# Routing in groups of 8, 8, 10 and 10 tiles, with earlier row writes and a reordered tail, in an attention and mixture-of-experts kernel

## The chip, the cores and the metric

One core of one Trainium2 chip. The metric is the device time of one execution in microseconds (us), given as the median of a few runs.

## The reference

Linear attention without a softmax, a norm per head, and then a mixture of eight experts that sends each token to one expert:

```python
kv = einsum('bhsd,bhse->bhde', k, v)             # batch 8, heads 8, seq 576, head_dim 64
out = einsum('bhsd,bhde->bhse', q, kv)
rms = sqrt(mean(out * out, axis=-1) + 1e-06)
x = (out / rms * g_norm)                          # reshaped to 4608 tokens x 512
logits = x @ w_gate                               # 8 experts
e_idx = argmax(logits, axis=1)
gate_w = softmax(logits)[e_idx]
eom = sigmoid(x @ w_output_gate)
for e in range(8):                                # w1: 512 x 1024, w2: 1024 x 512
    h = maximum(x[mask_e] @ w1[e], 0)
    out[mask_e] = gate_w * eom[:, e] * (h @ w2[e])
```

## The kernel before

The work has two phases. **Phase 1** is attention, gating and routing; **phase 2** is the experts. On TensorE, ScalarE, VectorE and GpSimd the order of phase 1 is the order of the program text (GpSimd's order is free in phase 2). SyncE issues the loads and the row writes, one behind the other, in program order too.

*Attention.* The 36 token tiles (128 tokens each) come out of eight batches. For a batch, five `kv_step`s (L486) sum k times v in PSUM; `kvT_part` (L510) and `m_part` (L522) fold the gate weights into it, so that one product gives a tile's attention output and its gate products together. `m_part` is the gate product; it writes the PSUM tile `mrp`. `run_out` (L785) makes one token tile: `out_tile` (TensorE, L576), for the tile before it `out_rows` (ScalarE: the row, its squares, the gate products), and for the one before that `sums` (VectorE, L602). Between these it issues loads (`load`, L468) as slots of a pool of 20 come free. Some `constant` matmuls (L484) on ones compute nothing that is used; their numbers stand in `COLD`.

*Routing.* The tiles are taken in groups, `GR`: 16, 10 and 10. When a group's last sum is there, the generator `route` (L614) begins. It has eight steps, each ended by a `yield`: (1) the inverse root of the sums, and on GpSimd its copy into the rows (L639); (2) gate products times it (L647); (3) logits, maximum, one-hot; (4) counts, and matmuls into `mrp` that number the tokens (L683 to L690); (5) two exponentials on ScalarE; (6) each token's slot, its output factor (the reciprocals, L723), and the writing of its rows to the HBM tensor `xs` (`xwrite`, L757 and L762); (7) the operands `la` and `rrc` of the tables (L733 to L739); (8) the table matmuls (L742), whose sum VectorE keeps in `tsum` (L744, L746). `STEPS` says after which token tile a group takes how many steps. Rows are written in chunks: tiles 0 to 7 in one, then two tiles each up to 25, then five and five. `xwrite` holds them back until all loads have been issued.

*The lead.* After 16 tiles the expert with most tokens so far is known. Its first 256 tokens are the lead, run 0: `gather(0)` (L243) reads its rows back from `xs` on GpSimd's queue, `scale_heads` (L259) multiplies in the norms on VectorE, `stage` (L267) transposes them (L283), `lead1` (L300, products at L308) is the first product in eight blocks, and the second is the part of `mm2` at L364. `HOOKS` puts the gather at tile 35. `TAIL` is the order by hand behind the 36 tiles: a digit is one step of that group, L one step of the lead (two tiles staged, then eight blocks), Q the last rows and sums, W the loads of the lead's second weights, C 8 `constant` matmuls, K the order of the other experts. So the last group's routing is interleaved with the lead's first product. Then come `index` (rows of run 1), `split` of the four chunks of the first expert's w1, and `others` (the other experts' rows).

*Experts.* Run 1 is the rest of the first expert, then come the other seven. Weights and tokens are each split into a rounded part and a remainder (`split`: rounded part on ScalarE at L218 or L225, remainder on VectorE at L221 or L228), and three products are summed. `mm1` (L313, matmuls at L329) is the first product in eight hidden blocks f, each emptied by ScalarE (L344) and VectorE (L345); the w2 chunks are split between these blocks. `mm2` (L352, L377 and L383) is the second product, with the next run's row tiles staged in it. Rows of a run are gathered on GpSimd's queue and scaled on GpSimd (L259), and outputs are scattered there (L394). An expert's loop for overflowing tokens at the end finds nothing to do here.

Of the kernel before, what the change touches and what calls it, by code (L numbers as in the profile page):

```python
# [25 lines left out]
E = 8  # L26
# [17 lines left out]

NOVER = NT + E

GR = (16, 10, 10)
GROUPS = [list(range(sum(GR[:i]), sum(GR[:i+1]))) for i in range(len(GR))]
GMAX = max(GR)

# [15 lines left out]

STEPS = [{18: 1, 19: 1, 20: 1, 24: 1, 25: 1, 26: 1, 27: 1, 31: 1},
         {29: 1, 30: 1, 31: 1, 36: 1}, {}]  # L70

PLACES = ['VP', 'VP', 'V']

HOOKS = {35: "G"}
TAIL = "Q11WCCCCLL2L2L2L221L2L1L2KLL2"

COLD = (24, (8, 8, 10, 5), 5, 4, 12, 8)

GPSIMD_GROUPS = 0
APART = (2,)  # L80


NORMS = "VV"

ROUND = 1.5 * 2.0 ** 30

# [39 lines left out]
def tiles_of(i):  # L126

    _, t0, n = RUNS[i]
    return [(t0 + k, k * P, min(P, n - k * P)) for k in range(-(-n // P))]
# [6 lines left out]
def body(ctx: ExitStack, tc: tile.TileContext, kvm, rem, qT, wg, gn, w1, w2, kc, xs, tab, out):  # L136
    nc = tc.nc
# [56 lines left out]
    def wload(p, which, c, eng=None):  # L194
        r = take([P, 1024], F32, "wraw")
        eng = eng or nc.sync
        src = (w1 if which == 1 else w2)[ds(expert(p, eng), 1), c]
        d = eng.dma_start(out=r, in_=src.rearrange("o p x -> p (o x)"))
        raw[(p, which, c)] = r
        return d  # L200
# [35 lines left out]
    xg, tails, xT, hT = {}, {}, {}, {}  # L236
# [19 lines left out]
    def scale_heads(x, eng):  # L256
        v = x[:, 0:DM].rearrange("p (h d) -> p h d", d=D)
        f = x[:, C_RMS:C_RMS + H].unsqueeze(2).to_broadcast([x.shape[0], H, D])
        eng.tensor_tensor(out=v, in0=v, in1=f, op=ALU.mult)  # L259

    def scale_rows(i):
        for k, (t, c0, M) in enumerate(tiles_of(i)):
            if i == 0 and NORMS[k] == "V":
                continue
            scale_heads(xg[(RUNS[i][0], t)][:M], nc.gpsimd)

    def stage(i, k):  # L267
        p = RUNS[i][0]
        t, c0, M = tiles_of(i)[k]
        x = xg.pop((p, t))  # L270
        if i == 0 and NORMS[k] == "V":
            scale_heads(x[:M], nc.vector)
        if k == 0:
            if i == 0:
                xT[i] = take([P, 4, LEAD], F32, "xT")
            else:
                xT[i] = [[mem.tile([P, 4, CMAX], F32R, name="xT", tag=f"xT{j}")] for j in range(2)]
        tl = cst.tile([P, 1], F32, name="tl", bufs=14)
        nc.vector.tensor_copy(tl[:M], x[:M, C_SCALE:C_SCALE + 1])
        tails[(p, t)] = tl  # L280
        ps = ps_b.tile([P, 2, 512], F32, name="tps", tag="big")[:, 0].rearrange("p (c m) -> p c m", c=4)
        for c in range(4):
            nc.tensor.transpose(ps[:, c, :M], x[:M, c * P:(c + 1) * P], ident[:M, :M])  # L283
        give(x)
        if i == 0:
            nc.scalar.activation(xT[0][:, :, c0:c0 + M], ps[:, :, :M], AF.Copy, scale=gcol[:, 0:1])
            return
        for j, (hi, lo) in enumerate(zip(*xT[i])):
            n = hi.shape[1]
            v = ps[:, j * n:(j + 1) * n, :M]  # L290
            nc.scalar.copy(hi[:, :, c0:c0 + M], v)  # L291
            nc.vector.tensor_tensor(out=lo[:, :, c0:c0 + M], in0=v,  # L292
                                    in1=hi.bitcast(F32)[:, :, c0:c0 + M], op=ALU.subtract)
# [107 lines left out]

    def lead_run():

        for k in range(len(tiles_of(0))):
            stage(0, k)
            yield
        for f in range(8):
            lead1(f)
            yield
# [70 lines left out]
    def constant(ps, n, start=True):  # L480

        for _ in range(n):
            k = ps.shape[1] // P
            nc.tensor.matmul(ps, ones, ones.unsqueeze(1).to_broadcast([P, k, P]), start=start, stop=start)  # L484

    def kv_step(b, s):  # L486

        r = rt[b // 2]
        q0 = (b % 2) * 64
        ps = kvp  # L490
        if s < 4 and b == 0:
            constant(ps[:, 256:512], COLD[1][s] + (COLD[0] if s == 0 else 0), s == 0)
        for p in range(NP):
            for u in range(2):
                c = slice(p * P + u * D, p * P + (u + 1) * D)
                if s < 4:
                    k, v = kvt[(b, s)][:, 0, c], kvt[(b, s)][:, 1, c]
                else:
                    k, v = r[q0:q0 + 64, 0, c], r[q0:q0 + 64, 1, c]

                nc.tensor.matmul(ps[u * D:(u + 1) * D, p * D:(p + 1) * D], k, v, start=(s == 0 and p == 0),
                                 stop=(s == 4 and p == NP - 1))
        if s < 4:
            give(kvt.pop((b, s)))
        elif b % 2:
            give(rt.pop(b // 2))
        if s == 4:
            nc.scalar.copy(augs[b % 3][:, :, 0:D], ps[:, 0:NP * D].rearrange("q (p d) -> q p d", p=NP))
# [30 lines left out]
    g = 0  # L539
# [214 lines left out]

    opened = [False, False]

    def xwrite(g, o, i):  # L757
        late = g >= LEAD_TILES
        if not opened[late]:
            xwrites.append((g, o, i))  # L760
            return
        nc.sync.dma_start(out=o, in_=i)  # L762
        if id(i) in held:
            give(i)
# [40 lines left out]
    def act(step):  # L805
        if step.isdigit():
            advance(int(step))
        elif step == "W":
            for c in range(4):
                wload(0, 2, c)  # L810
        elif step == "K":
            ranks()
        elif step == "Q":
            while outs:
                out_rows()
            while squares:
                sums()
        elif step == "G":
            free.extend(rfree)
            rfree.clear()  # L820
            gather(0)
        elif step == "C":
            constant(ps_b.tile([P, 2, 512], F32, name="cps", tag="big")[:, 0, 0:256], COLD[5])
        else:
            next(lead, None)
# [93 lines left out]
    with tc.manual_schedule(engines=MAN):  # L919
        p1_main()  # L920
        index()
        for c in range(4):
            split(0, 1, c)
        others()
    p1.close()

    def overflow_list():
# [67 lines left out]
    with tc.manual_schedule(engines={ET.PE, ET.Activation, ET.DVE}):  # L995
        for i in range(len(RUNS)):
            p = RUNS[i][0]
            T = len(tiles_of(i))
            last_run = i + 1 == len(RUNS)
            change = not last_run and RUNS[i + 1][0] != p  # L1000
            if i == 0:
                gather(1)
                scale_rows(1)
            else:
                for f in range(8):
                    mm1(i, f)
                    if f % 2:
                        split(p, 2, f // 2)
                        drop(1, f // 2)
                        if change:  # L1010
                            wload(p + 1, 1, f // 2)
                    if f == 2 and not last_run:
                        g_ = gather(i + 1)
                        if i + 2 == len(RUNS):
                            settle(g_)
                    if f == 3 and not last_run:
                        scale_rows(i + 1)
                    if i > 1:
                        next(listing, None)
            Tn = 0 if last_run else len(tiles_of(i + 1))  # L1020

            at = {}

            def put(k, f, e, *a):
                at.setdefault(k, {}).setdefault(f, []).append(lambda: e(*a))

            if change:
                for c in range(4):
                    at_ = (c, 0) if T >= 4 else divmod(c * T * 2, 8)
                    put(*at_, split, p + 1, 1, c)  # L1030
                    put(*at_, wload, p + 1, 2, c)
            places = [(k, f) for k in range(T) for f in (2, 5)]
            places = places[-Tn:] if Tn > len(places) - 2 else places[:-1]
            for x in range(Tn if i else 0):
                put(*places[x * len(places) // Tn], stage, i + 1, x)
            order = list(range(T))
            if last_run and half(i):
                order.insert(1, order.pop())
            for k in order:
                g_ = mm2(i, k, at.get(k, {}))  # L1040
                if last_run and k == order[-3]:
                    settle(g_)
            if i == 0:
                for h in hT.pop(0):
                    give(h)
                for k in range(Tn):
                    stage(1, k)
            if i > 0:
                for c in range(4):
                    drop(2, c)  # L1050
# [105 lines left out]
```

## Time and profile before

| | |
|---|---|
| median of 3 runs | 575.64 us (572.77 to 577.5) |
| the profiled execution | 577.09 us |
| its span, first to last instruction | 575.3 us |
| mean granted TensorE clock | 0.975 of full |
| TensorE matmuls busy | 560.7 us, 97% of the span |
| VectorE, ScalarE, GpSimd busy | 251.3, 220.1, 150.0 us |
| moved | 92.25 MB, mean 160 GB/s |
| row writes to `xs` | one of 2112 KB, nine of 528, two of 1320 |

Times are counted from the span's start. "Granted clock" is TensorE's, as a share of its upper level of 2.4 GHz; 0.5 is the lower level, 1.2 GHz. PE is TensorE, DVE VectorE, ACT ScalarE, POOL GpSimd, SPq SyncE's queue. A line such as `L221 DVE ... wlo<-wraw,gcol,whi` names the kernel's line, the engine, and output and inputs by tile names. In a line of the timeline the first two numbers are start and duration in us, `xN` is the number of instructions merged in it, and the bracket is the engine's idle time before it with what seems to have ended it. A busy share of TensorE is not its peak rate, as the ends of matmuls are modelled.

### The profile page before, as it was taken

How to read it: one execution, taken by the hardware profiler on the slowest of the kernel's cores; microseconds unless marked ns; L12 is line 12 of the kernel's file. 1: busy time of each engine (PE TensorE's matmuls, PEld its weight loads, DVE VectorE, ACT ScalarE, POOL GpSimd, SP SyncE). 2: the span in 40 equal slices, each digit the busy share in tenths (PEclk: the TensorE clock that was granted, in tenths of full speed). 3: DMA queues.
4: the chain of work that ended last, by engine and by line, in shares of the span. 5: the costliest groups of instructions: out<-in, count | busy, mean ns of one | idle time of the engine just before them, and what ended most of it. 6: DMA issues, size and time to landing. Idle time of an engine off the chain costs nothing.

```text
span 575.3 us, 10502 instructions
## 1 busy us (share of the span) xinstructions
PE 560.7 (97%) x4220; PEld 489.8 (85%) x4220; DVE 251.3 (44%) x519; ACT 220.1 (38%) x399; POOL 150.0 (26%) x168
## 2 busy tenths in 40 slices
PE   9899989998999999999999999999999999999995
PEld 6798978857988998899889988998799889879974
DVE  2033998872754563154413441353145425424400
ACT  1277765232452344134323432334235324433410
POOL 2000241348327005600450046005500631020011
PEclk9889995998999999999999999999999999999999
DMA  8999997966266223442254234323622443110000
GB/s 278 383 417 417 416 355 254 365 221 210 79 198 202 76 74 119 132 151 76 92 161 142 75 112 160 121 74 111 184 92 83 133 158 114 56 40 18 0 38 29
DMA packets 28739, 92.25 MB, mean 160 GB/s; under 512 B 4081, under 2 KB 4209, under 8 KB 28688
## 3 DMA queue, kind: packets, MB, share of 16 engines
q1 hardware_dynamic: 21952, 71.63, 35.1%
q0 software_dynamic: 6304, 19.70, 10.7%
q8 instruction: 35, 0.57, 0.4%
q10 hardware_dynamic: 432, 0.21, 0.2%
q14 instruction: 16, 0.13, 0.1%
HBM read 72.34 MB, written 19.70 MB: 160 GB/s over the span
## 4 chain that ended last, share of the span: by engine, by line
PE 77%; issue 1%; DVE 1%; ACT 1%; DMA 0%; POOL 0%; POOLq 0%
PE hps L329 34%; PE yps L383 32%; PE yps L377 3%; PE tps L283 3%; PE hps L308 2%; PE yps L364 2%; DVE wlo L228 1%; DMA out<-y,oidx 0%; DVE xT L292 0%; POOL out L394 0%; DVE hT L345 0%; ACT y L393 0%; ACT whi L225 0%; ACT hT L344 0%; POOLq L251 0%
## 5 line engine op out<-in xcount | busy, mean ns | idle before, releaser
L383 PE MATMUL yps<-whi,hT 128*128 128x512 f32 (+3 forms) x560 | 184.9, 398 | 0.0
L329 PE MATMUL hps<-xT,whi 128*128 128x256 f32 (+5 forms) x960 | 178.1, 305 | 0.9 <-ACT xT L291 0.4
L329 PEld LDWEIGHTS hps<-xT,whi 128*128 128x128 f32 x960 | 148.6, 189 | 3.0 <-DVE xT L292 0.6
L383 PEld LDWEIGHTS yps<-whi,hT 128*128 128x128 f32 (+3 forms) x560 | 104.0, 186 | 23.3
L394 POOL DMA_INDIRECT out<-y,oidx x42 | 45.7, 1089 | 258.1 <-ACT y L393 238.6
L383 PE MATMUL yps<-wlo,hT 128*128 128x512 f32 (+3 forms) x280 | 109.9, 393 | 0.0
L329 PE MATMUL hps<-xT,wlo 128*128 128x256 f32 (+5 forms) x480 | 109.7, 304 | 0.0
L345 DVE SCALAR_TENSOR_TENSOR hT<-hps,hT 128x512 fp32r<-128x512 f32 (+5 forms) x104 | 54.7, 526 | 116.8 <-ACT hT L344 116.7
L344 ACT ACTIVATE hT<-hps 128x512 fp32r<-128x512 f32 (+5 forms) x104 | 48.2, 467 | 140.7 <-PE hps L329 105.3
L329 PEld LDWEIGHTS hps<-xT,wlo 128*128 128x128 f32 x480 | 80.2, 189 | 0.4
L383 PEld LDWEIGHTS yps<-wlo,hT 128*128 128x128 f32 (+3 forms) x280 | 52.1, 186 | 10.7
L221 DVE SCALAR_TENSOR_TENSOR wlo<-wraw,gcol,whi 128x1024 fp32r<-128x1024 f32 x32 | 42.3, 1330 | 42.5 <-ACT whi L218 40.6
L259 POOL TENSOR_TENSOR xg<-xg 128x512 f32<-128x512 f32 (+8 forms) x40 | 44.4, 1118 | 38.5 <-DMA xg<-xs,gidx 29.2
L393 ACT ACTIVATE y<-yps,tl 128x512 f32<-128x512 f32 (+3 forms) x37 | 25.5, 689 | 75.5 <-PE yps L383 66.5
L243 POOL DMA_INDIRECT xg<-xs,gidx x42 | 42.1, 1002 | 43.2 <-PE yps L364 15.9
L228 DVE TENSOR_TENSOR wlo<-wraw,whi 128x1024 fp32r<-128x1024 f32 x32 | 41.8, 1307 | 16.9 <-ACT whi L225 14.6
L292 DVE TENSOR_TENSOR xT<-tps,xT 128x512 fp32r<-128x512 f32 (+8 forms) x40 | 25.3, 635 | 45.6 <-ACT xT L291 45.5
L576 PE MATMUL ops<-aug,ld 64*128 64x80 f32 (+1 forms) x640 | 45.2, 305 | 0.0
L291 ACT CAST xT<-tps 128x512 fp32r<-128x512 f32 (+8 forms) x40 | 21.5, 542 | 60.5 <-PE tps L283 60.5
L576 PEld LDWEIGHTS ops<-aug,ld 64*128 64x128 f32 (+1 forms) x640 | 39.8, 207 | 3.4 <-issue 1.5
L602 DVE TENSOR_REDUCE ss<-sq 128x8 f32<-128x512 f32 x36 | 23.9, 681 | 37.7 <-ACT sq L592 37.7
L218 ACT ACTIVATE whi<-wraw,gcol 128x1024 fp32r<-128x1024 f32 x32 | 36.3, 1143 | 0.0
(163 smaller groups left out, 443.2 us busy)
## 6 DMA issues: line engine op xcount, KB each, us to landing
wraw<-w SPq DMA_DIRECT2D x64, 512.0 KB, 3.5
ld<-kvm SPq DMA_DIRECT2D x32, 512.0 KB, 9.9
ld<-qT SPq DMA_DIRECT2D x18, 512.0 KB, 9.9
xs<-xrow SPq DMA_DIRECT2D x9, 528.0 KB, 5.9
xs<-xrow SPq DMA_DIRECT2D x2, 1320.0 KB, 7.8
xs<-xrow SPq DMA_DIRECT2D x1, 2112.0 KB, 9.3
ld<-rem SPq DMA_DIRECT2D x3, 512.0 KB, 9.9
xg<-xs,gidx POOLq DMA_INDIRECT x42, 3.6
```

The lines of the kernel that those rows point to most:

```text
L218: he.activation(hi, r, AF.Copy, scale=gcol[:, 0:1])
L221: eng.scalar_tensor_tensor(out=lo, in0=r, scalar=gcol[:, 0:1], in1=hi.bitcast(F32), op0=ALU.mult, op1=ALU.subtract)
L228: eng.tensor_tensor(out=lo, in0=r, in1=hi.bitcast(F32), op=ALU.subtract)
L243: gathered = nc.gpsimd.indirect_dma_start(out=x[:M, :], out_offset=None, in_=rows, in_offset=bass.IndirectOffsetOnAxis(ap=gidx[:M, p, t:t ...
L259: eng.tensor_tensor(out=v, in0=v, in1=f, op=ALU.mult)
L329: nc.tensor.matmul(ps[:, j, :n], w[:, o:o + P], x[d][:, j * N:j * N + n], start=(d == 0 and k == 0), stop=(d == 3 and k == 2))
L344: nc.scalar.activation(hh, x, AF.Relu)
L345: nc.vector.scalar_tensor_tensor(out=v(h[:, l:l + n]), in0=x, scalar=0.0, in1=hh.bitcast(F32), op0=ALU.max, op1=ALU.subtract)
L383: nc.tensor.matmul(ps[:M], a, b, start=(f == 0 and k == 0), stop=(f == 7 and k == 2))
L393: nc.scalar.activation(y[:M], ps[:M], AF.Copy, scale=tl[:M, 0:1])
L394: i_ = nc.gpsimd.indirect_dma_start(out=out, out_offset=bass.IndirectOffsetOnAxis(ap=oidx[:M, p, t:t + 1], axis=0), in_=y[:M], in_offset=N ...
L576: nc.tensor.matmul(v[r0:r0 + m, u, p, :], qt[g // 2][r, p, q0:q0 + m], augs[b % 3][r, p, :], start=True, stop=True)
```

## The change

The routing groups become 8, 8, 10 and 10. The lead is still made of the first 16 tiles, now the first two groups. The step tables move with that: the third group's first six steps run up to tile 34, before the tail, where the group of the same tiles had four by tile 36; the table matmuls of the first 16 tiles come at tiles 20 and 28 instead of 31. A hook E at tile 19 writes the rows of tiles 0 to 7 without waiting for the loads to be issued, and the lead's gather moves from tile 35 to 34. The last three `kv_step`s of batch 1 get 6, 5 and 3 `constant` matmuls. In the tail the lead's norms stand first, ahead of the last rows and sums, and two C (16 matmuls) replace four (32). `others` comes ahead of `split`, and only two w1 chunks are split there; the other two are split in run 1, behind its hidden blocks 0 and 2.

```diff
-GR = (16, 10, 10)
+GR = (8, 8, 10, 10)
...
-STEPS = [{18: 1, 19: 1, 20: 1, 24: 1, 25: 1, 26: 1, 27: 1, 31: 1},
-         {29: 1, 30: 1, 31: 1, 36: 1}, {}]
-PLACES = ['VP', 'VP', 'V']
-HOOKS = {35: "G"}
-TAIL = "Q11WCCCCLL2L2L2L221L2L1L2KLL2"
-COLD = (24, (8, 8, 10, 5), 5, 4, 12, 8)
+STEPS = [{10: 1, 11: 1, 12: 1, 14: 1, 15: 1, 16: 1, 17: 1, 20: 1},
+         {18: 1, 19: 1, 20: 1, 23: 2, 24: 1, 25: 1, 28: 1},
+         {28: 1, 29: 1, 30: 1, 32: 1, 33: 1, 34: 1}, {}]
+PLACES = ['VP', 'VP', 'V', 'V']
+HOOKS = {19: "E", 34: "G"}
+TAIL = "LCQWLLC3L3L3L332L3L2L3KLL3"
+COLD = (24, (8, 8, 10, 5), 5, 4, 12, 8, (0, 0, 6, 5, 3))
...
-APART = (2,)
-NORMS = "VV"
+APART = (3,)
...
     def lead_run():
+        for t, c0, M in tiles_of(0):
+            scale_heads(xg[(0, t)][:M], nc.vector)
+        yield
         for k in range(len(tiles_of(0))):
             stage(0, k)
             yield
...
     def kv_step(b, s):
+        if b == 1:
+            constant(ps[:, 256:512], COLD[6][s], False)
...
-    def xwrite(g, o, i):
+    def xwrite(g, o, i, wait=True):
         late = g >= LEAD_TILES
-        if not opened[late]:
+        if wait and not opened[late]:
             xwrites.append((g, o, i))
             return
...
+        elif step == "E":
+            for w in [w for w in xwrites if w[0] < 8]:
+                xwrites.remove(w)
+                xwrite(*w, False)
...
         index()
-        for c in range(4):
+        others()
+        for c in range(2):
             split(0, 1, c)
-        others()
...
                 for f in range(8):
                     mm1(i, f)
+                    if i == 1 and f in (0, 2):
+                        split(0, 1, f // 2 + 2)
```

## Rows read from the trace of the kernel before

**Rows 1.** Chain that ended last, in order of time: start, us, what.
```profile
102.96 5.45 PE hps L308 x24
...
118.42 13.82 PE yps L364 x32
...
135.86 6.39 PE hps L329 x23
...
144.58 3.83 DVE wlo L228
...
149.52 7.20 PE hps L329 x36
```
**Rows 2.** Timeline of GpSimd, 80 to 182 us.
```profile
90.83 1.09 POOL L243 DMA_INDIRECT xg<-xs,gidx  x1 [5.88 <-DVE ss L602]
...
92.22 0.95 POOL L243 DMA_INDIRECT xg<-xs,gidx  x1 [0.30 <-issue]
...
122.43 1.04 POOL L243 DMA_INDIRECT xg<-xs,gidx  x1 [15.63 <-PE yps L364]
...
131.52 2.05 POOL L259 TENSOR_TENSOR xg<-xg 128x512 f32<-128x512 f32 x2
...
142.28 7.03 POOL L259 TENSOR_TENSOR xg<-xg 128x512 f32<-128x512 f32 x6
```
**Rows 3.** Timeline of SyncE's queue, the row writes.
```profile
75.08 6.71 SPq L762 DMA_DIRECT2D xs<-xrow  x5
...
111.65 2.63 SPq L762 DMA_DIRECT2D xs<-xrow  x2
```
**Rows 4.** By tile, issue to landing: xs in 70 to 125, xg in 80 to 140.
```profile
DMA to landing us min/median/max: 2.9/5.6/10.1
...
DMA to landing us min/median/max: 3.1/4.4/5.0
```
**Rows 5.** Timeline of VectorE, 85 to 112 us.
```profile
86.54 0.17 DVE L749 CAST gidx<-gif 128x2 int32<-128x2 f32 x1
...
96.28 0.69 DVE L602 TENSOR_REDUCE ss<-sq 128x8 f32<-128x512 f32 x1 [1.02 <-ACT sq L592]
...
98.46 0.67 DVE L259 TENSOR_TENSOR xg<-xg 128x512 f32<-128x512 f32 x1
...
99.77 0.19 DVE L623 TENSOR_SCALAR ra<-ss 128x80 f32<-128x80 f32 x1
...
111.33 0.25 DVE L723 RECIPROCAL xrow<-rdn 128x5 f32<-128x5 f32 x2
```
**Rows 6.** Stretches: length, busy us of engines (instructions), PE clock, DMA share, GB/s.
```profile
74.00:76.00 2.00, 2.00 (x44) 1.85 (x44) 1.90 (x12) 2.00 (x7) 2.00 (x5) 1.00 0.44 175
76.00:92.00 16.00, 14.01 (x230) 12.88 (x230) 15.26 (x42) 10.12 (x25) 4.82 (x9) 0.80 1.03 374
```
**Rows 7.** Groups by line and shape, VectorE, 57 to 104: busy, mean ns | idle.
```profile
L631 DVE SCALAR_TENSOR_TENSOR ru<-ry 128x80 f32<-128x80 f32 x2 | 0.5, 243 | 0.1
...
L631 DVE SCALAR_TENSOR_TENSOR ru<-ry 128x128 f32<-128x128 f32 x1 | 0.3, 294 | 0.0
```
**Rows 8.** Stretches of phase 1 (busy: PE, PEld, DVE, ACT, POOL).
```profile
24.00:34.50 10.50, 10.44 (x136) 9.30 (x136) 2.65 (x4) 6.15 (x15) 0.00 (x0) 0.51 1.02 418
...
40.00:57.00 17.00, 17.00 (x360) 15.30 (x360) 6.38 (x10) 13.33 (x35) 0.00 (x0) 1.00 1.03 416
57.00:80.00 23.00, 23.00 (x495) 20.79 (x495) 22.00 (x63) 17.04 (x45) 7.79 (x13) 1.00 0.97 386
```
**Rows 9.** Waits of TensorE, 0 to 104 us: total, times, longest.
```profile
PE mrp L527 <- DVE tsum L744: 2.0, 1, 2.0
```
**Rows 10.** The stretch behind that wait.
```profile
85.77:95.06 9.29, 9.26 (x104) 8.83 (x105) 8.13 (x24) 6.96 (x16) 2.04 (x2) 0.50 0.99 349
```
**Rows 11.** The two remainder subtractions of weights: duration ns min/median/max, first and last start.
```profile
L228 DVE TENSOR_TENSOR wlo<-wraw,whi x32: 1224/1226/3832, 144.6 to 545.4; 128x1024 fp32r<-128x1024 f32 x32
...
L221 DVE SCALAR_TENSOR_TENSOR wlo<-wraw,gcol,whi x32: 1273/1285/1725, 120.0 to 510.9; 128x1024 fp32r<-128x1024 f32 x32
```

More of the change, by code (lines that the diff above doesn't have):

```diff
@@ L262, in scale_rows @@
         for k, (t, c0, M) in enumerate(tiles_of(i)):
-            if i == 0 and NORMS[k] == "V":
-                continue
             scale_heads(xg[(RUNS[i][0], t)][:M], nc.gpsimd)
@@ L270, in stage @@
         x = xg.pop((p, t))
-        if i == 0 and NORMS[k] == "V":
-            scale_heads(x[:M], nc.vector)
         if k == 0:
```

## The prediction

> **What bounds the kernel now.** I read the granted clock and busy time by stretch first, then the chain that ended last, then the queues of SyncE, GpSimd and VectorE one after the other in time.
>
> From 102.96 us the chain is TensorE with hardly a break: the lead's first product, its second from 118.42 for 13.82, then run 1 from 135.86, and after that the seven other experts [rows 1]. So nearly all of the time lies behind 136 us in matmuls that the change leaves alone. What it can move is the moment at which run 1 starts, and what run 1 then loses. Two breaks show in it: between the lead's end (132.24) and 135.86, and a VectorE subtraction of 3.83 us at 144.58 that the chain passes through [rows 1].
>
> What sets 135.86? Not the lead: GpSimd finishes scaling run 1's last two row tiles at 133.57 (131.52 plus 2.05), after the lead's last matmul [rows 1, 2]. GpSimd began that string (four gathers, four scalings, one output) at 122.43 and never waited in it. The gather at 122.43 needs every token row in HBM. The last two writes leave SyncE at 111.65, right behind the reciprocals that end at 111.58, and row writes land up to 10.1 us after issue [rows 3 to 5]; the second of the two, about a microsecond behind the first, fits that. So run 1 hangs on the last routing group, whose chain on VectorE begins at 99.77 and takes 11.8 us [rows 5]. In front of 99.77 stand the last sum (96.28), the end of the group before, and the lead's norms (98.46) [rows 5].
>
> The lead's own gather leaves at 90.83, though its index is ready at 86.7 [rows 2, 5]. It waits for the first 16 tiles' rows: writes issued from 75.08 for 6.71 us, landing up to 10.1 later [rows 3, 4]. Transfers are the limit there: share 0.44 in 74 to 76, then 1.03 until 92 [rows 6].
>
> **The change part by part.**
>
> *A fourth group.* The 28 or so small operations of a routing chain now run twice for the first 16 tiles. One takes 0.294 us on 128 columns and 0.243 on 80 [rows 7]; on 64 that is about 0.225 by the same slope, so 28 x (0.45 - 0.29) = 4.5 us more on VectorE. They fall at tiles 10 to 20, where VectorE works 6.38 us of 17 [rows 8]: cost 0 on the path, at worst 4.5 if they pile up behind the full stretch from 57 to 80 (22.00 of 23) [rows 8]. That full stretch loses half of the group of 16, by my count of its operations about 5.5 us. VectorE should therefore reach the lead's norms at about 91 to 92 instead of 98.46: 5.5 for this, and 1.3 for two sums that now come later.
>
> *Rows of tiles 0 to 7 at tile 19.* By the slot count only the last two q loads are still behind this write on SyncE; they land 5 to 6 us later, about 80, when tile 32 is due to need them. The bytes only change order, since the queue was full. What is won is the hole at 74 to 76: 2 x (1 - 0.44) = 1.1 us [rows 6]. The lead's gather goes from 90.83 to 89.7. Bounds: 0 (the hole comes back elsewhere) and 5.8, if its 2,112 KB (2.16 MB, at 374 GB/s [rows 6]) found free transfer time.
>
> *Dummy matmuls in batch 1 and the tables moved.* In 24 to 34.5 the clock was 0.51 [rows 8]. If the 14 dummies hold it, TensorE comes 3 to 5 us earlier to the loads, but the loads and the row writes do not end earlier: 0 on the path, bounds -3 and 0. The tables made the gate product wait 2.0 us for a VectorE copy [rows 9], and a stretch at 0.50 followed [rows 10]. Without it the last token tiles come earlier, but the lead's gather still waits for the writes: 0 again. The group before the last is ready by then, so its row writes no longer stand between norms and last group.
>
> *Norms ahead of the last sums, 16 dummies instead of 32.* The second lead gather follows the first by 1.4 [rows 2] and lands a median 4.4 us after issue [rows 4]: 89.7 + 1.4 + 4.4 = 95.5. Behind the waiting norm on VectorE stand the last two sums and the whole last group. Norm 0.67, two sums about 1.3 [rows 5]: the last group begins at 97.5 instead of 99.77, a gain of 2.3. Bounds: 6.0, if data are there and VectorE is the limit (92 + 0.67 x 2 + 1.3, less overlaps, 93.8); -1, if the gather lands at the 5.0 end and VectorE comes late. The lead's products start some 6 us earlier, about 97, which is hidden: run 1 waits for the last group, and TensorE idles before it some 3 us longer.
>
> *Two weight splits moved into run 1.* Before, all four w1 splits ran before run 1 under the lead's second product, and cost nothing. Now chunks 2 and 3 stand between run 1's first hidden blocks, on ScalarE and VectorE, with the product's own evacuations behind them. The subtraction takes 1.285 each [rows 11]. The ScalarE-VectorE chain there was already what TensorE waited for [rows 1], so I take 2 x 1.285 = 2.6 as lost. Bounds: 0 (slack between evacuations takes it) and 7.7 (both stretched as in the row of 3.83). What they free, VectorE and ScalarE time before run 1, only brings the index of run 2 forward, and GpSimd's string never waited for that.
>
> The row of 3.83 stands beside GpSimd's six scalings of 142.28 to 149.31 [rows 2]; the same subtraction's median is 1.226 [rows 11]. The Trainium skill (SBUF — State Buffer, Who interferes with whom) says that a VectorE instruction with two SBUF inputs and a GpSimd one that reads SBUF exclude each other for a whole instruction. By that rule the added subtractions, which also read two tensors, can be held up too, which speaks against the change and is the second rival below.
>
> *Sum.* -2.3 + 2.6 = +0.3. The profiled execution took 577.09 us (span 575.3), 1.45 above the median of the runs, 575.64. It would come to 577.4; by the median, 575.9, rounded 576.
>
> **The rivals.**
>
> A, faster: VectorE, not the gather, sets the last group, because half of the lead's rows were written long before. The last group begins at 93.8, 6.0 earlier, and the gaps between evacuations absorb the two splits: 575.6 - 6.0 = 569.6. For it: 4.3 MB of writes (16 tiles of 264 KB) stood in front of the lead's gather and only half still do. Against: the transfer engines had nothing free before 74, so the other half is not free either.
>
> B, slower: run 1's evacuations fall behind. Each added subtraction meets GpSimd's scaling and takes 3.83 instead of 1.285: 2 x 2.55 = 5.1 on top. TensorE then stands in holes as long as the 2.0 that was followed by 0.50 [rows 9, 10], and at least one hidden block (12 matmuls; 36 take 7.20 [rows 1], so 2.4, with the evacuations' holes left out 2.3) runs at half clock: 575.9 + 5.1 + 2.3 = 583. It decides from the point where two of the three subtractions in that window are held up. For it: one was. Against: GpSimd's string of 7 us is over by the time of the third.
> [...]
>
> C, the change does not do what it says: the norm blocks VectorE until the old landing time, the last group starts at 99.8, and only the splits are felt: 575.6 + 2.6 = 578.2. For it: gather and landing are the least certain times above. Against: the hole in the transfers is really there.
>
> **How the numbers follow.** Forecast 0.43, A 0.26, B 0.16, C 0.15. The forecast's own range is 573 to 579. The whole range takes in A, with a microsecond and a half below it, and most of B: 568 to 582.5. A measurement of this kernel can tell about 1% (5.8 us) from no change. Faster by more than that (under 569.9) is most of A, with a little of the forecast's lower end: 0.27. Slower by more (over 581.4) is B: 0.16. The rest 0.57.
>
> **What would show it.** In the changed kernel the lead's gather should issue near 89.7, its norms start near 94 with VectorE idle in front, the lead's first product near 97, the last group's chain near 97.5, run 1's gather near 120 and its first matmul near 133.5. TensorE should stand for 2 to 3 us in run 1 behind VectorE's evacuations, and batch 1 should show the full clock. I am wrong if run 1 starts before 131 (then A), if run 1's eight blocks take 5 us longer than the 20.9 of now, 135.86 to 156.72 [rows 1] (then B), or if the last group starts at 99 or later (then C).

## The result, and the profile after

| | before | after |
|---|---|---|
| median, same chip, side by side | 573.22 us (20 runs, from 572.71) | 579.01 us (20 runs, from 574.01) |
| profiled execution, its span | 577.09, 575.3 us | 579.98, 578.1 us |
| ratio, 95% interval | | 1.0063 [1.0036, 1.0090] |

The change costs 0.4 to 0.9% by the interval; the forecast was 576.0 (568 to 582.5) and no difference that can be told. The times of after lie at two levels, about 574 to 575 and 578 to 581. One run of the twenty on each side was in a slower state of the chip; medians, here and below, are over all runs, and ratios leave such runs out.

All of the difference lies ahead of run 1's second product: from there to the end of the span it is 418.6 us before (575.3 - 156.72 [rows 1]) and 418.0 after (578.1 - 160.05). The chain of waits of after, start, us, what:

```profile
90.96 7.21 DMA xg<-xs,gidx
98.19 0.69 DVE xg L260
98.88 1.19 DVE ss L604 x2
...
112.52 0.58 PE mrp L744 x10
113.10 5.25 PE hps L305 x24
...
118.78 12.96 PE yps L361 x30
131.76 0.44 ACT y L390
...
135.41 4.01 PE hps L326 x11
...
140.72 1.15 ACT whi L219
141.90 5.54 DVE wlo L222
...
148.54 11.52 PE hps L326 x48
160.05 2.07 PE yps L380 x9
```

Two things are new in it. The lead's gather itself is now on the chain, for 7.21 us, with the norms and the last two sums behind it; and the subtraction of a moved split takes 5.54 us where [rows 11] have 1.285. Run 1's products go on from 135.41 (one matmul at 134.65 stands alone ahead of them, as one at 135.10 did before). Beside [rows 1] (135.86) that is 0.45 earlier, which misleads, as the second experiment shows. The chain comes to run 1 over TensorE: the last group's table matmuls (112.52) stand ahead of the lead's last three blocks and its second product, and run 1 goes on 3.67 us behind the end of that product (131.74); before it was 3.62 (132.24 and 135.86). VectorE's timeline of after, the tail:

```profile
96.45 0.69 DVE L260 TENSOR_TENSOR xg<-xg 128x512 f32<-128x512 f32 x1 [7.25 <-DMA xg<-xs,gidx]
...
98.19 0.69 DVE L260 TENSOR_TENSOR xg<-xg 128x512 f32<-128x512 f32 x1 [1.05 <-DMA xg<-xs,gidx]
...
100.11 0.20 DVE L625 TENSOR_SCALAR ra<-ss 128x80 f32<-128x80 f32 x1
...
107.75 2.04 DVE L735 TENSOR_SCALAR la<-ni,rlon 128x128 bf16<-128x128 f32 x10
...
112.38 0.25 DVE L725 RECIPROCAL xrow<-rdn 128x5 f32<-128x5 f32 x2
```

VectorE reaches the first norm at 89.2 and stands 7.25 us in front of it, then 1.05 more. The last group begins at 100.11, behind the 99.77 of [rows 5]. GpSimd and SyncE's queue in the same time:

```profile
89.57 1.09 POOL L244 DMA_INDIRECT xg<-xs,gidx  x1 [9.87 <-DMA wraw<-w]
...
122.25 0.97 POOL L244 DMA_INDIRECT xg<-xs,gidx  x1 [18.65 <-DVE zf L886]
...
141.30 7.03 POOL L260 TENSOR_TENSOR xg<-xg 128x512 f32<-128x512 f32 x6
```
```profile
79.11 4.42 SPq L199 DMA_DIRECT2D wraw<-w  x4
87.92 4.38 SPq L764 DMA_DIRECT2D xs<-xrow  x5
92.54 4.86 SPq L199 DMA_DIRECT2D wraw<-w  x4
```

The gather leaves at 89.57 (90.83 in [rows 2]), and in front of it and between its two halves SyncE puts the five row writes of the third group, which before came only in the tail. By tile, in 88 to 96, issue to landing of the lead's two gathers of after, beside 4.0 to 4.7 before:

```profile
DMA to landing us min/median/max: 6.9/7.0/7.2
```

Stretches of after (columns as in [rows 6]): there is no hole in the transfers (share 1.04 where it was 0.44), the first stretch of [rows 8] has the full clock, and in the tail the transfers stay full. The first two of these need not be the work of the change: the second experiment shows them without it.

```profile
74.00:76.00 2.00, 2.00 (x51) 1.85 (x48) 1.76 (x10) 0.56 (x2) 0.00 (x0) 1.00 1.04 393
...
85.00:99.80 14.80, 8.36 (x62) 7.19 (x61) 6.37 (x23) 6.10 (x14) 2.04 (x2) 0.62 1.04 400
24.00:34.50 10.50, 9.96 (x210) 8.84 (x210) 3.43 (x5) 8.28 (x21) 0.00 (x0) 1.00 1.03 418
```

### The profile page after: what moved, and what is told of

It is laid out like the page before. It is cut to its first block, busy times and chain, and to the rows that moved or that the text cites. A ratio compares the mean times of both kernels' runs of the same rounds, so it can differ in the third digit from the quotient of the medians.

```text
span 578.1 us, 10543 instructions
## 1 busy us (share of the span) xinstructions
PE 556.8 (96%) x4221; PEld 485.5 (84%) x4221; DVE 259.4 (45%) x557; ACT 219.8 (38%) x401; POOL 142.9 (25%) x163
## 3 DMA queue, kind: packets, MB, share of 16 engines
q1 hardware_dynamic: 21952, 71.63, 34.5%
## 4 chain that ended last, share of the span: by engine, by line
PE 80%; DMA 12%; DVE 4%; issue 1%; ACT 1%; POOL 0%; POOLq 0%; ACTq 0%; DVEq 0%; SPq 0%
PE hps L326 34%; PE yps L380 32%; DMA ld<-kvm 5%; PE yps L374 3%; DMA xs<-xrow 3%; PE tps L280 3%; PE ops L578 3%; PE yps L361 2%; PE kvp L503 2%; DMA wraw<-w 1%; DMA xg<-xs,gidx 1%; DMA gcol<-gn 1%; DVE wlo L222 1%; PE hps L305 1%; DMA out<-y,oidx 0%
## 5 line engine op out<-in xcount | busy, mean ns | idle before, releaser
L222 DVE SCALAR_TENSOR_TENSOR wlo<-wraw,gcol,whi 128x1024 fp32r<-128x1024 f32 x32 | 47.8, 1498 | 43.8 <-ACT whi L219 42.0
L244 POOL DMA_INDIRECT xg<-xs,gidx x42 | 40.8, 971 | 50.1 <-DVE zf L886 18.7
L229 DVE TENSOR_TENSOR wlo<-wraw,whi 128x1024 fp32r<-128x1024 f32 x32 | 39.2, 1225 | 16.9 <-ACT whi L226 13.8
L578 PE MATMUL ops<-aug,ld 64*128 64x80 f32 (+1 forms) x640 | 41.4, 282 | 0.1
L578 PEld LDWEIGHTS ops<-aug,ld 64*128 64x128 f32 (+1 forms) x640 | 36.1, 187 | 3.2 <-issue 1.2
```

The source lines that it names most:

```text
L222: eng.scalar_tensor_tensor(out=lo, in0=r, scalar=gcol[:, 0:1], in1=hi.bitcast(F32), op0=ALU.mult, op1=ALU.subtract)
L229: eng.tensor_tensor(out=lo, in0=r, in1=hi.bitcast(F32), op=ALU.subtract)
L244: gathered = nc.gpsimd.indirect_dma_start(out=x[:M, :], out_offset=None, in_=rows, in_offset=bass.IndirectOffsetOnAxis(ap=gidx[:M, p, t:t ...
L578: nc.tensor.matmul(v[r0:r0 + m, u, p, :], qt[g // 2][r, p, q0:q0 + m], augs[b % 3][r, p, :], start=True, stop=True)
```

## The experiments

Two questions: how much each of the tail's new order and the moved splits costs, and what holds the lead's gather back. Medians below are of runs beside the kernel before on the same chip; the kernel before had 573.3 to 574.5 in them.

**The splits put back (the change's tail alone).** In the changed kernel `range(2)` is `range(4)` again and the two splits in run 1 go.

> The changed kernel with all four w1 splits ahead of run 1 again (after the other experts' rows), nothing else undone. Theory S (the loss is made in run 1, by the two added subtractions, one of which took 5.54 us beside GpSimd's scaling): run 1's first product, from its second matmul to the first of the second product, falls from 24.6 us (135.41 to 160.05) to about 21, and the time by 3 to 4 us, to the level of the kernel before or 0.5 under it, with less scatter. Theory T (the loss is made in the tail of phase 1, where the lead's second gather landed 7.2 us after issue and ten la operations stand on VectorE): run 1 begins where it does now and the time stays within 1 us of the changed kernel.

578.69 us, ratio 1.0088 [1.0063, 1.0114]: nothing is won. Run 1 starts at 136.22, and its chunk of w2 meets the scaling instead, in VectorE's and GpSimd's timelines:

```profile
143.37 6.13 DVE L229 TENSOR_TENSOR wlo<-wraw,whi 128x1024 fp32r<-128x1024 f32 x1 [0.72 <-ACT whi L226]
```
```profile
143.38 7.02 POOL L260 TENSOR_TENSOR xg<-xg 128x512 f32<-128x512 f32 x6
```

So the loss lies in the tail, with or without the moved splits: run 1 starts no earlier, as theory T had it.

**The split moved alone, in the kernel before.**

```diff
-        for c in range(4):
+        for c in range(2):
             split(0, 1, c)
...
+                    if i == 1 and f in (0, 2):
+                        split(0, 1, f // 2 + 2)
```

> The kernel before with the move of two w1 splits into run 1 as its only edit. Theory S: run 1's first product takes 3 to 4 us longer than its 20.9, and the time is 3 to 5 us above the kernel before. Theory T: within 1 us of the kernel before.

576.32 us (575.26 over the nine runs that the ratio counts), ratio 1.0023 [1.0005, 1.0041]: 0.3 to 2.4 us, under theory S's 3 to 5, and not clearly within the 1 of theory T. This kernel has the old tail, untouched, and shows what that does in an execution at the usual clock. Its timelines of VectorE and GpSimd:

```profile
95.50 0.69 DVE L259 TENSOR_TENSOR xg<-xg 128x512 f32<-128x512 f32 x1 [1.64 <-DMA xg<-xs,gidx]
...
96.84 0.19 DVE L623 TENSOR_SCALAR ra<-ss 128x80 f32<-128x80 f32 x1
...
137.12 6.62 DVE L221 SCALAR_TENSOR_TENSOR wlo<-wraw,gcol,whi 128x1024 fp32r<-128x1024 f32 x1 [0.83 <-ACT whi L218]
```
```profile
118.24 1.53 POOL L243 DMA_INDIRECT xg<-xs,gidx  x1 [14.38 <-DMA xs<-xrow]
...
137.60 7.02 POOL L259 TENSOR_TENSOR xg<-xg 128x512 f32<-128x512 f32 x6
```

The last group starts at 96.84 and run 1 at 132.22, not at the 99.77 and 135.86 of the profiled execution of before [rows 1, 5]. That one was some 4 us above its kernel's usual time: its stretch at a clock of 0.50 [rows 10] reads 0.82 here, on the same tail.

```profile
85.77:95.06 9.29, 7.92 (x85) 6.41 (x81) 7.61 (x30) 5.13 (x15) 2.04 (x2) 0.82 0.86 316
```

Beside this, the change starts run 1 3.2 us later (135.41 - 132.22). What remained of the early start here went into run 1's eight blocks, 24.99 us: TensorE waited 3.3 us in them, behind the subtraction of 6.62, and the clock stood at 0.50 from 144 to 150. Two more marks of the profiled execution of before are not found here, without the hook E and without dummies in batch 1:

```profile
24.00:34.50 10.50, 9.47 (x208) 8.43 (x208) 3.43 (x5) 7.32 (x18) 0.00 (x0) 1.00 1.02 415
74.00:76.00 2.00, 2.00 (x41) 1.77 (x39) 1.86 (x5) 1.68 (x5) 0.62 (x1) 1.00 1.04 409
```

So neither the clock of 0.51 in [rows 8] nor the hole at 74 in [rows 6] belongs to every execution of that kernel.

**The norms later.** TAIL "CQW333LLLCLLL332L3L2L3KLL3" puts the last rows, sums and three steps of the last group ahead of the lead's norms.

> The changed kernel with another tail: last rows and sums first, then the first three steps of the last group, and only then the lead's norms, so that VectorE works while it waits for the lead's gather (in the changed kernel it stood 7.25 us and then 1.05 more). Theory N (the norm ahead of the sums holds the last group back): the last group begins near 91 instead of 100.1, its reciprocals end near 106 instead of 112.6, run 1's gather goes near 116 and run 1 is then held by the lead's end, so it begins 1 to 3 us earlier; time 1 to 3 us below the changed kernel. Rival M (transfers hold run 1's gather: row writes land no earlier since the queue is full up to 104): run 1's gather still near 121 or later and the time unchanged.

578.46 us, ratio 1.0069 [1.0048, 1.0090]: no gain. The last group did start at 92.94, but the matmuls that number its tokens stood on TensorE behind the lead's blocks, and its reciprocals came at 111.09 (112.38 in after). Run 1's gather left at 121.69, where the rival had 121 or later, and run 1 started at 136.88, 3.67 us behind the lead's second product again. With the lead's blocks behind the same late gather, the order takes back what it gives.

**No dummies in batch 1.** `COLD[6]` is all zeros.

> The changed kernel without the 14 dummy matmuls of batch 1. The prediction put them at 0 on the path: the clock in 24 to 34.5 falls back to about 0.5, token tiles come up to 3 us later, the lead's gather still issues near 89.6, and the time stays within 1 us of the changed kernel. Rival (the dummies pay): the lead's gather and run 1 begin 2 us or more later and the time rises by that.

579.22 us (575.91 over the nine runs that the ratio counts), ratio 1.0046 [1.0011, 1.0081]. The interval overlaps that of the change: the dummies cost and win nothing that shows in the time. Without them the clock in 24 to 34.5 was 0.51 (before), 1.00 (the split moved alone) and 0.79 (here, in a profiled run of 586.52 us); with them it was 1.00 in all eleven profiles. So the dummies may hold the clock there, which three profiles without them don't settle.

**The third group's rows later.** Its sixth step goes back into the tail, behind the norms.

```diff
-         {28: 1, 29: 1, 30: 1, 32: 1, 33: 1, 34: 1}, {}]
+         {28: 1, 29: 1, 30: 1, 32: 1, 33: 1}, {}]
...
-TAIL = "LCQWLLC3L3L3L332L3L2L3KLL3"
+TAIL = "LCQ2WLLC3L3L3L332L3L2L3KLL3"
```

> The changed kernel, but the third group's sixth step (which issues the row writes of tiles 16 to 25) stands in the tail, behind the lead's norms and the last sums, as the group of the same tiles had it behind the sums. Theory G (these writes and the weight loads behind them share the transfer engines with the lead's gather, which therefore lands 7.2 us after issue instead of 4.4): the gather lands within 5 us, the second norm starts near 96 instead of 98.2, the lead's first product near 99 instead of 101.5, while the last group, which now waits for the sixth step too, begins near 99; run 1 begins no earlier than now, because the later row writes push the last ones back. Time within 2 us of the changed kernel. Rival (the gather is slow for another reason): the second norm still at 98 or later.

577.91 us, ratio 1.0082 [1.0051, 1.0112]; the gathers' landing only falls to 6.0 us, where theory G had 5, the second norm starts at 98.21, as the rival had it, and the last group at 101.76. The row writes leave at 101.63, but two loads of weights slid into their place:

```profile
80.10 7.30 SPq L199 DMA_DIRECT2D wraw<-w  x6
...
101.63 4.40 SPq L764 DMA_DIRECT2D xs<-xrow  x5
```

In this profile run 1's eight blocks took 20.7 us (135.64 to 156.32): no subtraction was stretched, and the first five of GpSimd's scalings took 7.5 us together instead of 5. TensorE had no wait for VectorE in them, so that the forecast's term of 2.6 for the splits is not to be seen there.

**Tables shared with GpSimd.** `PLACES[2]` is 'VP', so that four of the third group's ten `la` go back to GpSimd.

> The changed kernel with the table operands of the third group shared by VectorE and GpSimd, as the group of the same tiles had them; the change put all ten on VectorE. Theory P (the last group's chain on VectorE sets run 1): its reciprocals end 1.0 us earlier after its start (12.5 us now, 11.8 before), and run 1 and the time follow by about 1 us. Rival (the chain's end does not matter): time unchanged within 0.5 us.

579.58 us, ratio 1.0116 [1.0098, 1.0133]. The chain from the group's start to the start of its last reciprocals is 0.87 us shorter (11.40 against 12.27), as theory P had it. But the group began 0.69 us later (100.80), so that run 1's gather left only 0.18 earlier (122.07), and run 1 started at 136.02, 3.61 us behind the lead's second product (132.41). The time is no better; five runs of a kernel with two levels can't tell what the 0.87 is worth by itself.

**Without run 2's scaling.** `scale_rows` of run 2 is left out, so the norms of run 2's rows are missing from the output.

> The changed kernel without GpSimd's scaling of run 2's rows by their norms (that part is left out, nothing in its place). Theory L (VectorE's subtraction of two SBUF inputs cannot run beside GpSimd's string of scalings and ends only when the string does): the subtraction that took 5.54 us takes 1.28, TensorE's waits for VectorE in run 1 go from 2.0 to under 0.5, and run 1's first product falls from 24.6 to 20.5 to 22 us, the time by 3 to 4. Theory W (the added work itself fills ScalarE and VectorE): it stays above 23.5 and the time within 1 us.

575.18 us, ratio 1.0031 [1.0014, 1.0048], all 12 runs between 573.3 and 577.7: the level of 578 to 582 is gone. Run 1's eight blocks take 19.1 us with every subtraction at 1.23 to 1.31. Run 1 still starts at 135.70. So the upper level goes with the scaling, as theory L had it, and the late start is something else. Run 1's blocks of after and of this kernel:

```profile
135.41:160.05 24.64, 22.63 (x96) 20.67 (x97) 14.46 (x19) 9.05 (x18) 11.67 (x11) 0.86 0.41 129
```
```profile
135.70:154.81 19.11, 19.11 (x96) 18.13 (x97) 10.48 (x19) 9.04 (x18) 4.61 (x5) 1.00 0.50 167
```

The 5.5 us between them are not the subtraction alone. TensorE waited 2.0 us for VectorE in after, and a mean clock of 0.86 over 24.64 is an estimated 3.4 us more.

**The changed kernel once more**, in the same group of runs as the three before.

> The changed kernel once more, to see another execution: its times lay at two levels, about 574.5 and 579.5. If the clock decides between them, an execution of the lower level shows no stretch at 0.5 in run 1 or before it where the upper one has 6.83 + 6.83 + 3.41 + 3.41 us of them; if the collision of the subtraction with GpSimd's scaling does, it shows a subtraction of under 2 us in run 1's first hidden block. From run 1's second product to the end both take 418 us, as in all profiles so far.

579.03 us, ratio 1.0082 [1.0050, 1.0114]; last group at 100.91, run 1 at 136.32, 3.67 us behind the lead's second product. The profile fell on the upper level again, so that none of a lower one was seen; that such an execution has no meeting of subtraction and scaling is inferred from the kernel without scaling. It does speak against the clock in run 1 as what makes the upper level:

```profile
136.32:159.08 22.76, 19.54 (x96) 17.88 (x97) 14.18 (x19) 8.99 (x18) 12.71 (x11) 1.00 0.42 139
```

The subtraction of the first hidden block took 1.28 us here, which the expectation had as a sign of the lower level; the next one then met the scaling and took 5.19.

**The tail's old order, and with it the old splits.** The third group's sixth step is back in the tail, TAIL has the order of the kernel before (the group's fifth step still runs ahead of it), and `la` is shared as there; the second kernel also has all four splits ahead of run 1. Both keep the 14 dummies of batch 1, which their expectations call missing.

```diff
-         {28: 1, 29: 1, 30: 1, 32: 1, 33: 1, 34: 1}, {}]
-PLACES = ['VP', 'VP', 'V', 'V']
+         {28: 1, 29: 1, 30: 1, 32: 1, 33: 1}, {}]
+PLACES = ['VP', 'VP', 'VP', 'V']
...
-TAIL = "LCQWLLC3L3L3L332L3L2L3KLL3"
+TAIL = "Q2WCCCCLLL3L3L3L332L3L2L3KLL3"
```

> The changed kernel with the tail's order and planes of before: the third group's first five row blocks are written in the tail and no longer between loads, the lead's two norm blocks stand behind the group's last sums again, four of the ten la planes go back to GpSimd; groups of 8, 8, 10, 10, the early sixth step of the first two groups, the missing batch-1 dummies and the moved weight splits stay. Theory (the tail's order holds the last group back): the lead's gather lands within about 5 us of its issue, the last group starts near 97 instead of 100.1, run 1's first matmul near 132.5 instead of 135.4; what is left beside before is the moved splits, so the time is that of the split moved alone, 575 to 577. Rival (groups of 8, or the early steps of the first two groups, cost it themselves): run 1 starts at 135 or later all the same, and the time stays at 578 to 579.

> As the kernel with the tail's old order, and with all four weight splits ahead of run 1 as before; of the change there are left the groups of 8, 8, 10, 10, the early sixth step of the first two groups and the missing batch-1 dummies. Theory (everything that the change costs is the tail's order and the subtractions beside GpSimd's scaling): run 1 starts near 132.5 and its eight blocks of the first product take 19 to 21 us, so the time is that of before, 573 to 574.5. Rival (the groups cost something themselves): 576 or above, with run 1's first matmul at 135 or later.

579.83 us, 1.0092 [1.0059, 1.0125], and 577.50 us, 1.0043 [1.0012, 1.0074]. Half of the theory held: the last group starts at 96.95 and 96.99. But run 1 started no earlier, about 7 us behind the end of the lead's second product. The reason is in GpSimd's timeline of the second:

```profile
122.72 1.70 POOL L391 DMA_INDIRECT out<-y,oidx  x1 [18.72 <-ACT y L390]
124.73 0.99 POOL L244 DMA_INDIRECT xg<-xs,gidx  x1 [0.31 <-issue]
```

GpSimd's order in phase 2 is not written by hand, and in these two kernels it came out with the scatter of the lead's first output ahead of run 1's gathers (the first likewise, at 122.68 and 124.06). That output exists only at 122.7. The edit had brought an order of its own with it, so neither run speaks for or against the groups.

**The same two with the gathers first.** One edge more: the lead's scatters stand behind run 1's gathers on GpSimd, as in the kernels before and after.

```diff
-                gather(1)
+                rows1 = gather(1)
...
                 g_ = mm2(i, k, at.get(k, {}))
+                if i == 0:
+                    tc.add_manual_dep(g_.ins, rows1.ins.name,
+                                      mybir.DependencyInfo(mybir.DependencyClass.NoSync,
+                                                           mybir.DependencyReason.DATA),
+                                      reason="order of GpSimd")
```

> The kernel with the tail's old order and all four splits ahead of run 1, and one edge more: the scatter of the lead's first output tile stands behind run 1's four gathers on GpSimd, as in the kernels before and after. In the run without the edge the last group started at 96.99 and its reciprocals at 108.38, but GpSimd had the scatter first in its order, which waited for the lead's output until 122.72, and run 1's gathers only left at 124.73. Theory (the tail's order is the whole loss before run 1, and the groups of 8 cost nothing): run 1's first gather leaves near 118.2, run 1's first matmul near 132 to 132.5, and the time is 573 to 574.5, the ratio 0.998 to 1.001. Rival (the groups or the early row writes cost something): run 1 still starts at 134 or later, time 576 or above.

> As the kernel before it here, but with two of the splits moved into run 1, as in the change: what is left of the change is the groups, the early writes, the batch-1 dummies and the moved splits; the tail's order is that of before. Theory (tail about 3.2, splits 0 to 4 by whether VectorE is held by GpSimd's scalings): run 1's first matmul near 132 to 132.5, its second product near 152 to 157, and the time 574.5 to 576.5. Rival (the splits cost nothing): 573 to 574, equal to the kernel with the splits ahead of run 1.

Old splits: 572.40 us, ratio 0.9970 [0.9950, 0.9990], a little better than expected. Moved splits: 576.14 us, ratio 1.0022 [0.9997, 1.0047]. Timelines of the first, VectorE, GpSimd and SyncE:

```profile
95.19 1.35 DVE L260 TENSOR_TENSOR xg<-xg 128x512 f32<-128x512 f32 x2 [1.65 <-DMA xg<-xs,gidx]
96.58 0.19 DVE L625 TENSOR_SCALAR ra<-ss 128x80 f32<-128x80 f32 x1
```
```profile
118.72 1.04 POOL L244 DMA_INDIRECT xg<-xs,gidx  x1 [15.13 <-DVE tbl L915]
```
```profile
79.95 4.56 SPq L199 DMA_DIRECT2D wraw<-w  x4
93.43 4.55 SPq L764 DMA_DIRECT2D xs<-xrow  x5
98.22 3.86 SPq L199 DMA_DIRECT2D wraw<-w  x4
```

The row writes now leave behind both halves of the gather, which lands 4.6 us after its issue, and the last group is where it was with the untouched tail. In the profile of the second, run 1 starts at 131.85, where 132 to 132.5 was expected. The first's profile fell on the longest of its twelve executions (574.07): there run 1 starts at 133.85, behind a lead whose first three blocks took 8.15 us instead of 5.45 at a clock of 0.76, so that its start doesn't tell the theories apart, and the time does:

```profile
93.00:107.00 14.00, 10.21 (x47) 8.13 (x48) 11.44 (x41) 2.71 (x7) 4.51 (x7) 0.76 1.00 359
```

The ledger, in ratios to before. Groups, early writes, dummies, the earlier gather and the other rows ahead of the splits, without the tail and the moved splits: 0.9970. With the moved splits: 1.0022, so these cost 0.5%, about 3.0 us (3.7 by the medians); in the kernel before they cost 1.3 us by the ratio. With the new tail instead (TAIL, the third group's sixth step and its `la`), splits back: 1.0088, so the tail costs 1.2%, nearly 7 us, of which the profiles account for about 6 (run 1 from about 132 to 136.22, and 21.8 us for its blocks with a subtraction at 6.13, against 20.26). Each of these ratios is uncertain by 0.2 to 0.3%. With both, the change itself: 1.0063 to 1.0082; the two losses don't add, since with the splits back the chunk of w2 meets the scaling in their place.

## Why the prediction was near, and where it failed

The number fell into the range, and no difference over 1% was the likeliest forecast; the difference itself, +0.3, was missed: it is +5.8 by the medians, +3.6 by the ratio. That 576 came within 3 us of 579.01 is in part luck. The base of 575.64 was 2.4 too high, which made up for nearly half of what the sum missed; from 573.22 the same sum comes to 573.5.

*What bounds it.* Right that run 1's start hangs on the last group, wrong on the way ("not the lead"). The way through row writes and gather is there: from the group's start to run 1's gather it is 22.1 us after (122.25 - 100.11), and 21.3 to 22.7 in [rows 2, 5] and all other kernels with the gathers first but that with the norms later (28.8). But it is the second by a little. In eleven of the fourteen profiles, that of before among them, run 1 goes on 3.61 to 3.67 us behind the end of the lead's second product, though GpSimd's scalings ended 0.28 us behind that end in the kernel with the split moved alone (128.89 and 128.61) and 1.33 in before (133.57 and 132.24). The lead's products wait on TensorE for the last group's table matmuls, and at their start for the lead's gather.

*The base.* Wrong. The steps were subtracted from marks of an execution at 577.09 whose tail ran in part at half clock; the median shown was 575.64 of three, and of twenty 573.22. An early start that the change seemed to bring was that execution's lateness, and the hole at 74 and the clock in batch 1, which the change was to mend, are not in the other execution with the old phase 1 either. Against the usual tail, 97.5 for the last group would have been no gain at all: it starts at 96.84 there.

*The early rows of tiles 0 to 7.* The 1.1 us is not shown. The gather leaves at 89.57 in this profile (the forecast had 89.7), but at 90.01 to 90.92 in ten others with the same hook (94.57 in the profiled run of 586.52 us), against 90.83 before and 90.87 with the split moved alone, where nothing is written early and there is no hole.

*VectorE early at the norms.* Right, and earlier than forecast: 89.2 (the text had 91 to 92). This is why rival A fell: VectorE was free, the data were not there. The fourth group shows no cost on the path, as forecast; 128 by 64 took 225 ns.

*Landing 4.4 us after issue.* This is the step that failed. It was a median of gathers on an emptier queue. The change itself moved 2640 KB of row writes (five of 528) from behind the gather to in front of it and between its halves, by taking the third group's sixth step before the tail; the forecast counted this as a relief ("no longer stand between norms and last group") and didn't price what is queued ahead of the gather. It took 6.9 to 7.2 us, and 6.6 to 7.2 in the five other profiles with the writes there. With the writes behind it, 3.5 to 4.7 (seven profiles); with two weight loads in their place, 6.0. Since the norms stood ahead of two sums and the last group on VectorE, the 2.6 us more went straight into the path: 97.5 plus 2.6 gives the 100.11.
That was rival C's condition (99 or later), and C's time, 578.2, is the nearest to the result; but C put it down to the old landing time, where it was a new and longer one.

*The chain of the last group.* 0.7 us longer than taken, 12.5 (112.63 - 100.11) instead of 11.8. The third group's ten `la` all fall on VectorE in it (2.04 us at 107.75), a line of the diff that the forecast passed over.

*The moved splits, 2.6.* The size was near (3.0 to 3.7 with the old tail), the mechanism not: it is no 1.285 twice. Nor did TensorE stand for the ScalarE-VectorE chain before: in run 1 it waited for it 0.2 us in all, beside the subtraction of 3.83. Where no subtraction is stretched, run 1's blocks take 19.1 to 20.7 us; where the scaling is met, one subtraction takes 2.4 to 6.6. This is rival B's mechanism, its second half included: behind the wait of 2.0 us in after the clock stood at 0.50 from 150 to 152. Its price is smaller, run 1's blocks being 3.8 us longer than before where B had 7.4 on top of the 2.6. By the two levels of the times the meeting comes in some executions and not in others.
The Trainium skill (SBUF — State Buffer, Who interferes with whom) says that such a VectorE instruction and a GpSimd one that reads SBUF exclude each other, and that whoever issues first gets the ports for a whole instruction. The exclusion agrees with the runs (5.54 us beside the scalings, 1.31 without them); but the subtraction was held over several of GpSimd's instructions, and who wins does not follow the starts in the profile, as the last section shows.

*Dummies and tables.* Nothing that shows, as forecast. The 2.0 us wait of [rows 9] is gone. In its place TensorE waits for the norms and for the third group's numbering, in the waits of after, 80 to 165 us:

```profile
PE tps L280 <- DVE xg L260: 6.4, 2, 5.9
PE hps L326 <- DVE hT L342: 2.0, 1, 2.0
PE mrp L690 <- DVE ohb L672: 1.7, 1, 1.7
```

*The lead, "hidden".* Its first product came at 101.49, not 97, and with the old tail it came at 98.36 (the split moved alone): the new tail made it 3.1 us later, as it made run 1. In after it stayed hidden by 0.9 us, TensorE's wait for the last group ahead of the table matmuls at 112.52. In the profile of the changed kernel once more it came at 102.58 by the chain, behind the same late gather, and there was no such wait: there the chain goes through the lead's first product itself. In 85 to 99.8 the clock was 0.62 in after and 0.50 in that profile.

## What to carry to other kernels

A wait put at the head of an in-order engine takes on the landing time of its data, and that time must be priced with the queue as the change leaves it: bulk transfers that the same change moves ahead of the awaited one count. Compare a profiled execution with the median before its marks are used as a base; a kernel with the stretch untouched is a better base than one odd profile. When an edit is undone for an experiment, look first whether an order that nobody wrote has moved with it; here that hid an improvement of 5.1 us by the medians (577.50 to 572.40), about 4.2 by the ratios. The version to keep has the groups of 8, the early writes and the earlier gather, with the old tail, the old splits and that one edge: 572.40 us. Where its last microsecond or two against before come from was not separated; groups, early writes and gather went together.

## What the runs showed of the hardware

- A gather of 128 rows landed 3.5 to 4.7 us after its issue, and 6.0 to 7.2 with five row writes of 528 KB or two weight loads of 512 KB queued in front. Of two stretches of the tail, the one with the longer landing moved 400 GB/s (85 to 99.8, after), the other 345 (the same, in the kernel of 572.40).
- VectorE's subtraction and GpSimd's string of six scalings: in after the first five took 1042 ns each, as if alone, and the last, of 16 rows, 2013; the subtraction began 0.60 us behind the string and ended 0.90 before its end. The same 0.88 to 0.90 stands in ten other profiles, that of before among them (148.41 and 149.31 by [rows 1, 2]), and also where the subtraction began first (137.12 against 137.60). With the tables shared, both were longer (2.63 and 8.04). Where the third group's rows came later, it was the other way: the subtractions took 1.28 and 1.31, and GpSimd's first five 1529 ns each. By form, in 135 to 155 us, after and then that kernel:

```profile
L260 POOL TENSOR_TENSOR xg<-xg 128x512 f32<-128x512 f32 x5 | 5.0, 1042 | 0.0
...
L260 POOL TENSOR_TENSOR xg<-xg 16x512 f32<-16x512 f32 x1 | 2.0, 2013 | 0.0
```
```profile
L260 POOL TENSOR_TENSOR xg<-xg 128x512 f32<-128x512 f32 x5 | 7.5, 1529 | 0.0
...
L260 POOL TENSOR_TENSOR xg<-xg 16x512 f32<-16x512 f32 x1 | 1.0, 1034 | 0.0
```

What decides which of the two waits was not found.

- TensorE's clock behind a wait in run 1 differed between executions. After a wait of 2.0 us (after), 3.3 (the split moved alone) and 2.5 (moved splits with the gathers first) it stood at 0.50 for 3 to 6 us; after one of 2.5 us (the splits put back, and the changed kernel once more) it stayed at 1.00.
